# One batch row's decays through DRAM instead of TensorE, and a new written-out order, in a gated linear attention with a bilinear feed-forward layer

## The chip, the cores and the metric

The kernel runs on one core of a Trainium2 chip. TensorE (PE) multiplies matrices, VectorE (DVE), ScalarE (ACT) and GpSimd (POOL) work elementwise, SyncE (SP) issues transfers. The metric is the device time of one execution in microseconds (us).

## The reference, cut to what matters

Per batch row and head a 48 x 48 state is decayed, updated and read at each of 768 positions; the eight heads' outputs, side by side, go through a bilinear layer.

```python
# q, k, v, alpha: (4, 8, 768, 48); w_a, w_b: (384, 1536); w_out: (1536, 384)
for t in range(768):
    state = alpha[:, :, t, :, None] * state + k[:, :, t, :, None] * v[:, :, t, None, :]
    y[:, :, t] = (q[:, :, t, None, :] @ state)[..., 0, :]
x = y.transpose(0, 2, 1, 3).reshape(3072, 384)
out = ((x @ w_a) * (x @ w_b)) @ w_out
```

## The kernel before

**Chunks.** The work is cut into six chunks. Chunk `c` holds the 256 positions of third `c // 2` for two of the four batch rows, which are its rows `u` = 0 and 1. A partition holds two neighbouring positions (`r` = 0, 1), so a row is 128 partitions, and these are two halves `g` of 64 partitions. The recurrence is solved half by half: scores within a half, and a state carried from half to half.

**Attention, per row.** `la` is the logarithm of alpha and `l2` its sum over the two positions of a partition. A product with a triangular matrix gives running sums of `l2` in PSUM (`B` for chunk 0, which starts from `la` itself, `A2` elsewhere); ScalarE turns them into `beta` (their exponential) and `invb` (that of the negative sum) (`E`). VectorE multiplies q by `beta` and k by `invb` into `QKp` (`mq`, `mk`). `QKp` is transposed to `kqT`, by TensorE (`C`, evicted by `Ce`) in chunks 0 and 1 and by a transposing DMA (`T`) in the others. Scores are `D`, their masks `M`, or `Mc` and `Mm` in two steps, what a half adds to the state `K`, the state's update `k` (lines L758 to L762), the outputs from the state `SA` and `SB`, those from the scores `Y`, and `X` evicts the result as `xT`.

**The decay.** The update `k` of half `g` multiplies the state by the exponential of that half's whole sum, a number for each head and each of 48 rows of the state, with the rows on partitions (tile `bl`, two buffers that chunks take in turn). There are two ways to get it. In chunks 0 and 1, `dk` (L687) lets TensorE sum `l2` (in chunk 0: `la`) over the partitions of each half, one 48 x 2 product per head and row, and `de` (L692) takes the exponential. In chunks 2 to 5 the last partition of each half of `beta` already holds the numbers, in a row: `dr` (L671) writes them to DRAM by two transfers and `dl` (L676) reads them back, four bytes at a time, with the rows of the state on partitions, by two more. All four are issued by SP.

**The bilinear layer, per chunk.** `a f w` and `b f w` (L851) are the products of `xT` with block `f` of 12 of `wa_t` and `wb_t`, for one row (`w` = 0, 1, 256 columns) or both (`*`, 512 columns), three matmuls each. ScalarE copies `a` out of PSUM (`as`, L857), VectorE multiplies it by `b` into `prod` (`pr`, L865). `o m half` (L873) are six matmuls each with `wo_t`, `ot` evicts, `st` stores; the last block of tokens is done in two column halves (`oc`, `otc`, `stc`, L884).

**The order.** Nothing is scheduled by the compiler. `PROGRAM` is a list of such steps, each with its chunk; each engine runs its own instructions in the order of the list, and waits by semaphores for its operands and for the buffers that it writes. A digit at the end of a step that fills PSUM is the first of the banks that it takes, out of eight; a final letter names the engine: V VectorE, S ScalarE, P GpSimd, Y SP. Where it stands on a load (`ld`, of q, k, v or alpha as `a`), it is the queue that issues the transfer. `W` and `Wo` load the weights on GpSimd's queue. `fill n i` is `n` matmuls of zeros that nobody reads, put in to keep TensorE at work, and `cz`, `cs`, `cu`, `ci`, `cm` prepare constants. The list weaves the attention of a chunk into the bilinear layer of the chunk before.

Of the kernel before, what the change touches and what calls it, by code (L numbers as in the profile page):

```python
# [17 lines left out]
0: ld a 0b Y; cm 0; cz 0 q P; cz 0 b P; c1; cs 0 m V; c1a; ld a 0a Y; ld k 0b Y; ld q 0b Y; cu; ld q 0a Y; fill 7 6; cu2 P; ld v 0 P; cus; ld a 1 P; ln 0b  # L18
0: B 0b 5; ln 0a; ci; ld q 1 P; B 0a 0; E 0b i; E 0b b; ld k 0a Y; cz 1 b P; ld k 1 P; dk 0 3; mk 0b V; mq 0b V; E 0a b; C 0 1 4; cm 1; ld v 1 P; E 0a i
0: mq 0a V; W b 0 256; fill 3 1; mk 0a V; Ce 0 1 S; C 0 0 0; v 0 V; de 0; D 0 1 6; Ce 0 0 V; K 0 0 5; k 0 0 V; W a 0 256; M 0 1; D 0 0 4; SB 0 0; ln 1; W a 256 768  # L20
0: cz 0 v V; W b 256 768; M 0 0; B 1a 2
1: ld a 0 P
0: cs 1 0 P
1: ld a 1 P
0: B 1b 6; E 1a i; E 1a b; mq 1a V; mk 1a V; W a 768 1536; dk 1 5; E 1b i; C 1 0 2; de 1; v 1 S; mk 1b V; SA 0; Y 0; Ce 1 0 V; W b 768 1536; D 1 0 3
1: ld k 0 P
0: E 1b b; K 1 0 5; cs 1 m V; mq 1b V; X 0 S
1: ld v 0 P
0: K 0 1 2; C 1 1 6; a 0 0 0; a 1 0 7; Mc 1 0; k 0 1 V; Ce 1 1 V; k 1 0 V; a 2 0 3; as 1 0
1: ld q 0 P  # L30
0: cs 0 0 P; b 1 0 1; D 1 1 6; as 0 0; SB 1 4; Mm 1 0 V; as 2 0; Mc 1 1; a 3 0 0; pr 1 0; a 4 0 2; c2 P; Wo 0 6; cz 1 q V; Wo 6 12; b 2 0 3; pr 2 0; Mm 1 1 V
0: as 3 0; b 0 0 6; b 4 0 1; b 5 0 7; pr 0 0; Y 1; SA 1; K 1 1 6
1: ln 0
0: as 4 0
1: l2 0 V; ld k 1 P
0: X 1 S; b 3 0 0; a 5 0 2
1: ln 1
0: a 5 1 4; a 4 1 5; pr 3 0; pr 4 0; as 5 0; a 3 1 0; b 5 1 3
1: l2 1 V
0: pr 5 0; as 4 1; b 4 1 2; as 5 1; a 1 1 5; b 1 1 1; pr 4 1  # L40
1: ld q 1 P
0: cz 1 v P
2: ld a * P
0: as 1 1; a 6 * 4; as 3 1; pr 1 1
1: ra 0
0: a 0 1 0; a 2 1 7; a 8 * 1; b 3 1 2; pr 5 1; k 1 1 V
1: H 1 V; H 0 S
0: as 6 *
1: L 1 V
0: b 2 1 3; a 11 * 5; pr 3 1  # L50
1: L 0 V
0: a 7 * 6
1: ld v 1 P
0: as 11 *; b 6 * 2; as 2 1; pr 6 *; b 11 * 7; a 10 * 4
1: ra 1
0: as 0 1; pr 2 1
1: v 0 V
0: pr 11 *; as 7 *
1: lv 0 k P; A2 0 2
2: ld k * P  # L60
0: b 0 1 0
1: A2 1 5
0: as 8 *; b 7 * 3
1: lv 0 q V
0: pr 0 1
2: ld q * P
1: E 1 i; E 0 b
0: pr 7 *
1: E 1 b; E 0 i; mq 0 V
0: b 10 * 6; b 9 * 1; a 9 * 7; as 9 *; as 10 *  # L70
1: mk 0 V
0: b 8 * 0
1: dk * 5
0: pr 8 *; pr 10 *; pr 9 *
1: C 0 1 3; C 0 0 4
0: o 3 0 0
1: Ce 0 1 S; de *; Ce 0 0 V; K 0 0 7; D 0 0 4; k 0 0 V; K 0 1 3; D 0 1 1; Mc 0 0; lv 1 k P; SB 0 6; M 0 1
0: o 3 1 -
1: mk 1 V
0: o 0 0 5; ot 3 S  # L80
2: ln *
1: lv 1 q V
2: ld v * P
3: ld a * P
0: o 0 1 -
1: mq 1 V
0: o 2 0 4
1: Mm 0 0 V; k 0 1 V; C 1 0 2
0: o 1 0 0
1: Ce 1 0 V; v 1 V  # L90
2: l2 * V
0: ot 0 S; o 1 1 -
2: ra 0
1: SA 0
0: ot 1 S
2: H * S
1: D 1 0 1; K 1 0 3
2: lv 0 k P
1: M 1 0; Y 0
0: o 2 1 -  # L100
1: X 0 S; C 1 1 5
0: ot 2 S
1: a 5 0 6
2: L * V
1: Ce 1 1 V
2: lv 1 k P
1: a 3 0 1; k 1 0 V; as 3 0; a 1 0 0; as 5 0; b 1 0 7; b 3 0 2; as 1 0
2: A2 1 1
1: pr 3 0
2: ra 1  # L110
3: ld k * P
1: pr 1 0; SB 1 5
2: E 1 i
1: D 1 1 3; K 1 1 2; M 1 1
2: lv 1 q P; lv 0 q P; E 1 b
1: a 11 0 0
2: A2 0 7
1: as 11 0; b 11 0 1
2: E 0 i
1: b 5 0 0; pr 11 0  # L120
2: E 0 b
1: a 4 0 4; pr 5 0; a 0 0 3
2: dr
1: a 6 0 1; k 1 1 V; as 4 0; as 0 0; a 2 0 0; b 4 0 7
2: mk 1 V
1: as 6 0; b 6 0 3; pr 6 0; a 7 0 1; b 0 0 2; pr 4 0; b 7 0 4; pr 0 0; a 9 0 3; as 9 0
2: mq 1 V
1: as 2 0; SA 1; Y 1; as 7 0
2: T 1
1: b 9 0 2; X 1 S; pr 7 0; a 8 0 3; pr 9 0; b 2 0 0; as 8 0  # L130
2: v 1 S
1: b 8 0 1; pr 2 0; a 10 0 4; b 10 0 2
3: lv 0 k P
1: a 0 1 0
2: mq 0 V
1: as 10 0; a 9 1 5; as 0 1; pr 10 0; a 5 1 6
4: ld a * P
1: b 5 1 7
3: ln *
1: b 0 1 3; pr 8 0; a 2 1 0  # L140
2: dl
3: lv 1 k P
1: as 5 1; pr 0 1; a 1 1 2; b 1 1 4; as 1 1; pr 5 1; as 9 1; b 9 1 3; pr 1 1; as 2 1; a 8 1 6
2: mk 0 V
1: a 4 1 7; b 2 1 1
2: v 0 S
1: as 4 1; pr 9 1; a 11 1 2; b 11 1 0; b 4 1 5; pr 2 1; b 8 1 3; pr 4 1; as 8 1; pr 8 1
3: l2 * V
1: a 3 1 4
2: T 0  # L150
1: as 11 1; a 7 1 1; b 3 1 6
0: st 3 Y
1: o 2 0 5; a 10 1 7; as 7 1
3: ld q * Y
1: pr 11 1; as 3 1
0: st 1 Y
1: as 10 1; pr 3 1
2: D 1 0 3; K * 0 1; Mc 1 0; D 1 1 6; k * 0 V
1: a 6 1 0; b 7 1 2
3: ra 1  # L160
2: Mc 1 1
1: pr 7 1
5: ld a * Y
1: b 10 1 3; o 2 1 -; as 6 1
3: ra 0
0: st 0 Y
1: b 6 1 4; ot 2 S; pr 10 1
2: Mm 1 0 V; D 0 0 2; K * 1 1
3: H * V
1: pr 6 1; o 3 0 0  # L170
2: Mc 0 0; k * 1 V; Mm 1 1 V; SB 0 4; SB 1 6
3: L * V
2: D 0 1 2
3: lv 1 q P
1: o 0 0 1
2: Mc 0 1
1: o 3 1 -
2: Mm 0 0 V
4: ln *
3: A2 1 3  # L180
2: Mm 0 1 V; SA 1
3: ld v * P
4: ld v * P
2: Y 1; Y 0; X 1 V; SA 0
3: A2 0 2
2: X 0 S
3: E 0 b
1: o 0 1 -
3: lv 0 q V; E 1 b; E 0 i; mk 0 V
1: ot 3 S  # L190
3: E 1 i
2: b 5 * 6; b 3 * 4; a 4 * 5; a 5 * 7
1: ot 0 S
3: mq 1 V
2: a 3 * 2; a 2 * 1
3: dr
2: a 1 * 3; as 5 *; b 0 * 7; as 3 *; b 1 * 0; as 1 *
3: v 1 V
2: pr 5 *; pr 3 *; as 2 *
1: st 0 Y; st 3 Y  # L200
4: ld q * P
3: dl
2: b 2 * 3
3: mq 0 V
2: a 6 * 1
3: T 0
0: st 2 Y
2: as 6 *; pr 1 *
4: l2 * V; H * V; ra 1
2: as 4 *; b 4 * 2; a 11 * 0; b 6 * 6; a 0 * 4; b 8 * 1  # L210
1: o 1 0 5
4: L * V
2: pr 2 *; pr 6 *
3: v 0 V
2: as 0 *; a 8 * 3; pr 4 *; as 11 *; pr 0 *
3: mk 1 V
2: b 11 * 2; a 7 * 6; as 8 *; pr 11 *
1: o 1 1 -
2: pr 8 *
3: T 1  # L220
1: st 2 Y
3: K * 0 2
1: ot 1 S
3: k * 0 V
4: ld k * Y
1: st 1 Y
3: K * 1 0; D 0 0 3
2: as 7 *
3: Mc 0 0
2: b 9 * 1  # L230
3: k * 1 V
2: a 9 * 7
5: ld k * Y
2: b 10 * 5; as 9 *; a 10 * 6; b 7 * 3; pr 9 *; as 10 *; o 0 0 0; pr 7 *; pr 10 *
3: D 1 1 6; D 1 0 1
4: lv 1 k P
3: M 1 1
2: o 0 1 -
3: Mc 1 0
5: ld q * P  # L240
3: Mm 1 0 V; SB 0 3
2: ot 0 S
3: SB 1 1; D 0 1 5
4: lv 1 q V; A2 0 0
2: o 2 0 7
3: Mc 0 1
4: ra 0; lv 0 k V
5: ln *
4: E 0 b
3: Mm 0 1 V  # L250
2: o 3 0 6
3: Mm 0 0 V
5: lv 1 k P
4: lv 0 q P
5: ld v * P
3: Y 1; SA 0; Y 0; SA 1
2: o 3 1 -
3: X 0 S; X 1 V
2: o 2 1 -
4: mq 0 V; A2 1 2  # L260
2: ot 2 S
3: a 2 * 5
5: l2 * V
3: b 4 * 3
4: E 1 b; E 0 i; E 1 i
3: b 3 * 4; a 4 * 7; b 2 * 2
4: v 1 S
3: as 2 *
4: dr
5: H * S  # L270
2: ot 3 S
5: ra 0
2: st 0 Y
4: mk 0 V
3: as 4 *
4: mk 1 V
2: st 2 Y
3: a 8 * 1
4: T 0
3: a 1 * 0; a 0 * 6; b 8 * 7; as 8 *; b 5 * 5; pr 2 *; pr 4 *  # L280
4: v 0 V; dl
5: lv 0 q V
3: pr 8 *
4: mq 1 V
5: lv 0 k V
3: as 0 *
5: ra 1
3: a 3 * 1; a 5 * 3; b 0 * 7; a 9 * 6; as 5 *; pr 5 *; a 7 * 3; a 11 * 5; pr 0 *; as 9 *; as 3 *; as 1 *
4: T 1
3: b 9 * 6; b 1 * 1  # L290
5: lv 1 q V
3: pr 9 *; a 6 * 2; pr 3 *; as 11 *; pr 1 *; as 6 *
4: K * 0 0; D 0 0 4
5: L * V
3: as 7 *; b 11 * 6; b 6 * 7; pr 11 *; a 10 * 1; pr 6 *
4: Mc 0 0
2: o 1 0 5
3: as 10 *
4: k * 0 V; D 1 0 3; D 1 1 6; D 0 1 1
5: v 1 S  # L300
4: Mc 1 0; M 1 1
5: A2 0 0
2: o 1 1 -
4: SB 0 6; Mc 0 1; Mm 0 0 V; SB 1 3
2: ot 1 V
5: A2 1 2
3: b 7 * 1
5: E 1 i; E 1 b; E 0 b
3: b 10 * 5
4: Mm 0 1 V; Mm 1 0 V  # L310
3: pr 7 *; o 1 0 2
5: mk 1 V
3: pr 10 *; o 2 0 1
5: mq 1 V
4: Y 1; SA 0
5: dr
2: st 3 Y
5: T 1
4: Y 0; SA 1; X 1 S
5: E 0 i  # L320
3: o 1 1 -; o 2 1 -
4: X 0 V
5: mk 0 V; mq 0 V
3: ot 1 S
4: a 6 * 0; a 7 * 5; as 6 *
5: T 0
4: b 6 * 3; as 7 *; a 1 * 6
5: dl
4: pr 6 *; a 0 * 5; b 7 * 7; pr 7 *
3: ot 2 V; st 1 Y  # L330
4: as 0 *; as 1 *; a 5 * 3; b 1 * 4; b 0 * 2
2: st 1 Y
3: st 2 Y
4: pr 1 *; as 5 *; pr 0 *
5: v 0 V
4: a 3 * 0; a 4 * 7; as 3 *
5: D 0 0 5
4: as 4 *
5: K * 0 4; M 0 0; D 1 1 2; D 1 0 0; Mc 1 1
3: o 3 0 7  # L340
5: k * 0 V; Mc 1 0
3: o 3 1 -
5: SB 1 5
3: ot 3 S
5: SB 0 3; D 0 1 0
4: b 10 * 2
3: o 0 0 7
5: M 0 1; Mm 1 0 V; Mm 1 1 V
4: b 3 * 1; b 4 * 0
3: o 0 1 -  # L350
4: pr 4 *; b 5 * 0
3: ot 0 S
5: SA 1
4: pr 5 *
5: Y 1; Y 0
4: pr 3 *
5: X 1 V; SA 0
4: a 2 * 7; a 10 * 6
5: X 0 S
4: as 10 *; as 2 *; a 8 * 5  # L360
5: a 4 * 3
4: b 2 * 0
3: st 0 Y
5: a 2 * 4
4: pr 2 *; as 8 *; a 9 * 7
5: b 2 * 1; a 11 * 0
4: pr 10 *; b 8 * 5
5: as 2 *; as 4 *; a 1 * 4
4: b 9 * 2; pr 8 *
5: pr 2 *; b 5 * 3; b 1 * 6  # L370
4: as 9 *
5: b 4 * 1; a 8 * 5
4: a 11 * 7
5: pr 4 *
4: pr 9 *
5: b 11 * 1; as 11 *; as 1 *; a 5 * 4; a 0 * 2; pr 11 *; pr 1 *; as 0 *; as 5 *; b 0 * 0; b 7 * 6
4: o 0 0 1; as 11 *
# [31 lines left out]
def kernel(  # L409
# [14 lines left out]
    C = 128  # L424
# [599 lines left out]
```

## Time and profile before

| | |
|---|---|
| median of 3 runs | 196.53 us (195.69 to 196.65) |
| the profiled execution | 196.2 us, of which the profile's span is 194.4 us |
| PE busy | 189.4 us (97%), 2582 matmul records |
| DVE, ACT, POOL busy | 133.2, 106.4, 50.6 us |
| mean granted TensorE clock | 0.999 |
| moved by DMA | 29.40 MB in 57034 packets |

Times in the views count from the span's start. Matmul records are pipelined: one lasts longer than the distance to the next, so stretches of the chain of waits, which follow each other without overlap, are what costs are taken from. A group of the profile carries a line of the kernel and the tiles written and read. A matmul of 32-bit operands leaves two records in `dk` (two passes), so 16 of its matmuls are 32 records.

### The profile page before, as it was taken

To read this page: it belongs to the slowest core of one execution; us is meant where nothing else is said; L and a number is where in the kernel's file an instruction comes from. 1 tells how busy PE (TensorE), PEld (TensorE's weight loads), DVE (VectorE), ACT (ScalarE), POOL (GpSimd) and SP (SyncE) were. 2 spreads that over 40 slices of the span, in tenths; PEclk is the share of its full clock that TensorE was granted. 3 is DMA by queue.
4 is the path that set the end of the run, shared out by engine and by line. 5 is a ranking of instruction groups with operands and counts; after the bars stand their busy time and mean duration, and the time that the engine had idled before them with its cause. 6 is when DMAs were issued, how large, how long until landed. Compare 5 with 4: busy or idle time off the path is not lost.

```text
span 194.4 us, 5977 instructions
## 1 busy us (share of the span) xinstructions
PE 189.4 (97%) x2582; PEld 119.6 (62%) x2582; DVE 133.2 (69%) x221; ACT 106.4 (55%) x197; POOL 50.6 (26%) x69
## 2 busy tenths in 40 slices
PE   7999999999999999999999999999999999999993
PEld 3988875566888876644557544557455644445562
DVE  2498777988998879579786777996585525543311
ACT  4458784655859777645547684863462253431311
POOL 8999749160727004400004500000000000000000
PEclk9999999999999999999999999999999999999999
DMA  5999999999976999998699599007850100000342
GB/s 145 270 210 220 244 240 229 261 254 263 246 199 113 189 200 303 141 281 165 113 291 231 82 205 146 1 3 72 177 138 0 44 3 0 0 0 0 129 146 95
DMA packets 57034, 29.40 MB, mean 151 GB/s; under 512 B 47560, under 2 KB 54600, under 8 KB 57008
## 3 DMA queue, kind: packets, MB, share of 16 engines
q0 software_dynamic: 19056, 15.73, 44.0%
q1 hardware_dynamic: 37808, 13.19, 32.3%
q8 instruction: 20, 0.33, 0.7%
q10 hardware_dynamic: 144, 0.10, 0.2%
q14 instruction: 6, 0.05, 0.1%
HBM read 25.98 MB, written 4.74 MB: 158 GB/s over the span
## 4 chain that ended last, share of the span: by engine, by line
PE 96%; DVE 1%; issue 1%; ACT 0%; DVEq 0%
PE psum L851 48%; PE psum L873 24%; PE psum L797 7%; PE psum L773 3%; PE psum L744 2%; PE psum L628 2%; PE psum L707 2%; PE psum L571 2%; PE psum L588 2%; PE psum L589 2%; PE psum L687 1%; PE psum L884 1%; DVE kqT L715 0%; DVE m L786 0%; DVE prod L865 0%
## 5 line engine op out<-in xcount | busy, mean ns | idle before, releaser
L851 PE MATMUL psum<-xT,wb_t 128*128 128x512 bf16 (+1 forms) x270 | 56.0, 337 | 0.0
L851 PE MATMUL psum<-xT,wa_t 128*128 128x512 bf16 (+1 forms) x270 | 55.5, 337 | 0.0
L873 PE MATMUL psum<-wo_t,prod 128*128 128x384 bf16 x276 | 49.5, 326 | 0.0
L851 PEld LDWEIGHTS <-wa_t 128*128 128x128 bf16 x270 | 25.9, 98 | 19.6 <-issue 0.2
L851 PEld LDWEIGHTS <-wb_t 128*128 128x128 bf16 x270 | 25.7, 98 | 19.9 <-issue 0.6
L873 PEld LDWEIGHTS <-prod 128*128 128x128 bf16 x276 | 26.0, 98 | 18.2 <-issue 0.5
L888 ACT ACTIVATE ot<-psum 128x384 f32<-128x384 f32 (+1 forms) x20 | 9.5, 480 | 20.4 <-PE psum L873 16.1
L642 POOL TENSOR_TENSOR k_t<-k_t,a_t 128x384 f32<-128x384 f32 x8 | 8.5, 1069 | 38.7 <-DMA k_t<-in_k_dram 36.0
L782 ACT ACTIVATE m<-psum 128x1024 bf16<-128x1024 f32 x15 | 15.1, 1022 | 4.3 <-PE psum L773 4.3
L778 DVE TENSOR_TENSOR m<-psum,mask 128x1024 bf16<-128x1024 f32 x9 | 11.0, 1217 | 3.4 <-PE psum L773 3.3
L832 ACT ACTIVATE xT<-psum 128x768 bf16<-128x768 f32 x8 | 6.5, 810 | 9.6 <-PE psum L797 9.5
L554 ACT ACTIVATE la<-a_t 128x1536 f32<-128x1536 f32 (+2 forms) x9 | 9.5, 1054 | 3.5 <-DMA a_t<-in_alpha_dram 3.4
L786 DVE TENSOR_TENSOR m<-m,mask 128x1024 bf16<-128x1024 bf16 x15 | 11.2, 765 | 0.1
L666 DVE TENSOR_TENSOR QKp<-k_t,invb 128x768 bf16<-128x768 f32 x10 | 9.4, 951 | 2.3 <-issue 1.5
L797 PE MATMUL psum<-m,vx 64*64 64x128 bf16 x576 | 10.3, 217 | 0.2 <-DVE m L786 0.2
L773 PE MATMUL psum<-kqT 64*64 64x128 bf16 x384 | 10.0, 219 | 0.3 <-DVE Sm L758 0.2
L666 DVE TENSOR_TENSOR QKp<-q_t,beta 128x768 bf16<-128x768 f32 x10 | 9.7, 972 | 0.2
L797 PEld LDWEIGHTS <-vx 64*64 64x64 bf16 x576 | 9.0, 107 | 1.0 <-issue 0.8
L547 POOL DMA_DIRECT2D v_t<-in_v_dram x8 | 8.4, 1053 | 0.1
L773 PEld LDWEIGHTS <-kqT 64*64 64x64 bf16 x384 | 6.9, 106 | 2.4 <-issue 2.0
L797 PE MATMUL psum<-kqT,Sm 64*64 64x128 bf16 x144 | 7.9, 220 | 0.0
L642 POOL TENSOR_TENSOR q_t<-q_t,ra 128x384 f32<-128x384 f32 x4 | 4.1, 1024 | 14.1 <-DMA q_t<-in_q_dram 12.8
(262 smaller groups left out, 286.2 us busy)
## 6 DMA issues: line engine op xcount, KB each, us to landing
out_dram<-ot SPq DMA_DIRECT2D x23, 192.0 KB, 2.9
a_t<-in_alpha_dram POOLq DMA_DIRECT2D x3, 768.0 KB, 13.9
q_t<-in_q_dram POOLq DMA_DIRECT2D x3, 768.0 KB, 9.2
k_t<-in_k_dram POOLq DMA_DIRECT2D x2, 768.0 KB, 12.1
v_t<-in_v_dram POOLq DMA_DIRECT2D x4, 384.0 KB, 7.1
k_t<-in_k_dram SPq DMA_DIRECT2D x2, 768.0 KB, 6.6
a_t<-in_alpha_dram POOLq DMA_DIRECT2D x3, 384.0 KB, 8.9
q_t<-in_q_dram POOLq DMA_DIRECT2D x3, 384.0 KB, 13.5
```

The lines of the kernel that those rows point to most:

```text
L547: eng.dma_start(out=t[:, us, hs].rearrange("p b h r d -> p (b h) (r d)"), in_=src[ch.b0 + us.start:ch.b0 + us.stop, hs, ch.s * 2 * C:(ch.s ...
L554: nc.scalar.activation(out=ch.la[:, us, hs].rearrange("p b h r d -> p (b h r d)"), in_=ch.a[:, us, hs].rearrange("p b h r d -> p (b h r d) ...
L642: eng.tensor_mul(x, x, by)
L666: eng.tensor_mul(QKp[ch.c % 2][:, u, j, :, hs, :D], src[:, u, hs].rearrange("p h r d -> p r h d"), f)
L773: nc.tensor.matmul(s2[g * HC:(g + 1) * HC, r, p, rk, :], lhsT=ch.kqT[u][rs, 1, rk, 2 * h + p, g * HC:(g + 1) * HC], rhs=queriesT(ch, u, 2 ...
L778: nc.vector.tensor_mul(m.rearrange("p r a k s -> p (r a) (k s)"), ch.s2[u, h].rearrange("p r a k s -> p (r a) (k s)"), maskn(4))
L782: nc.scalar.activation(out=m.rearrange("p r a k s -> p (r a) (k s)"), in_=ch.s2[u, h].rearrange("p r a k s -> p (r a) (k s)"), func=AF.Copy)
L786: eng.tensor_mul(x, x, maskn(4))
L797: nc.tensor.matmul(y[c * DP:(c + 1) * DP, g, j // 2 * C:(j // 2 + 1) * C], lhsT=lhsT, rhs=rhs, start=(g, c) not in begun, stop=False, skip ...
L851: nc.tensor.matmul(p, lhsT=(wa_t, wb_t)[w][:, kk, f * 128:(f + 1) * 128], rhs=ch.xT[:, kk, us, :], start=(kk == 0), stop=(kk == KT - 1))
L873: nc.tensor.matmul(op, lhsT=ch.prod[:, f, at:at + C], rhs=wo_t[:, f, :], start=(f == 0), stop=(f == NFF - 1))
L888: nc.scalar.activation(out=o_, in_=i_, func=AF.Copy)
```

## The change

The decays of chunk 1 are split by row. Row 0 keeps the way through TensorE (`dk 0`, `de 0`, 8 matmuls, 16 records, where `dk *` had 16 matmuls, 32 records). Row 1 gets its decays by `dr 1` and `dl 1`: two transfers of one row of 384 numbers out of `beta`, and two of 48 x 8 numbers back. So that a row's decays lie together, the DRAM tile `row` and `bl` are laid out with the row first and the half second, and `dr`, `dl`, `de` and the update `k` address them so; chunks 2 to 5 still take both rows at once.

`PROGRAM` as a whole is another order of the steps. Apart from `dk`, `de`, `dr` and `dl` it holds the same attention and bilinear steps, some of them on another engine or queue or with the mask in the other form, and `fill 7`, `fill 3` have become `fill 5`, `fill 3`. Other functions that are added or changed (`rest`, `top`, `cum_quads`, `const_utb`) are called by no step of the list, and chunk 0 takes the same path through `expo` and `mul` as before.

```diff
 (the first steps, up to the first products of the bilinear layer)
-0: ld a 0b Y; cm 0; cz 0 q P; cz 0 b P; c1; cs 0 m V; c1a; ld a 0a Y; ld k 0b Y; ld q 0b Y; cu; ld q 0a Y; fill 7 6; cu2 P; ld v 0 P; cus; ld a 1 P; ln 0b
-0: B 0b 5; ln 0a; ci; ld q 1 P; B 0a 0; E 0b i; E 0b b; ld k 0a Y; cz 1 b P; ld k 1 P; dk 0 3; mk 0b V; mq 0b V; E 0a b; C 0 1 4; cm 1; ld v 1 P; E 0a i
-0: mq 0a V; W b 0 256; fill 3 1; mk 0a V; Ce 0 1 S; C 0 0 0; v 0 V; de 0; D 0 1 6; Ce 0 0 V; K 0 0 5; k 0 0 V; W a 0 256; M 0 1; D 0 0 4; SB 0 0; ln 1; W a 256 768
-0: cz 0 v V; W b 256 768; M 0 0; B 1a 2
...
-0: B 1b 6; E 1a i; E 1a b; mq 1a V; mk 1a V; W a 768 1536; dk 1 5; E 1b i; C 1 0 2; de 1; v 1 S; mk 1b V; SA 0; Y 0; Ce 1 0 V; W b 768 1536; D 1 0 3
...
-0: E 1b b; K 1 0 5; cs 1 m V; mq 1b V; X 0 S
...
-0: K 0 1 2; C 1 1 6; a 0 0 0; a 1 0 7; Mc 1 0; k 0 1 V; Ce 1 1 V; k 1 0 V; a 2 0 3; as 1 0
+0: cm 0; ld a 0b Y; ci; cz 1 b P; c1a; c1; cz 0 b V; cz 0 v V; cu; cu2 P; ld a 0a Y; fill 5 3; ld v 0 P; ld q 0b Y; ld k 0b Y; ln 0b; cus; ln 0a; B 0b 6
+0: cz 1 v V; cz 0 q V; cz 1 q V; E 0b b; E 0b i; B 0a 4; dk 0 6; ld a 1 P; ld q 1 P; ld k 1 P; ld k 0a Y; mk 0b V; E 0a b; mq 0b V; E 0a i; ld q 0a Y; mk 0a V
+0: C 0 1 7; cm 1; cs 0 m P; mq 0a V; fill 3 0; C 0 0 1; de 0; Ce 0 1 S; v 0 V; D 0 1 6; Ce 0 0 V; ld v 1 P; cs 0 0 P; ln 1; W a 0 256; K 0 0 3; k 0 0 V; W b 0 256
+0: D 0 0 2; SB 0 0; M 0 1; W a 256 768; cs 1 m P; W b 256 768; Mc 0 0; B 1a 4
...
+0: E 1a b; B 1b 2; dk 1 7; mq 1a V; mk 1a V; Mm 0 0 V; C 1 0 6; E 1b b; W a 768 1536; W b 768 1536; K 0 1 5; mq 1b V; E 1b i; Y 0; v 1 V; SA 0; mk 1b V; Ce 1 0 S
+0: de 1; C 1 1 4; D 1 0 6; k 0 1 V; Ce 1 1 V; X 0 S; Mc 1 0; K 1 0 5; a 1 0 0; k 1 0 V; as 1 0; a 0 0 4; D 1 1 2; SB 1 6; b 1 0 1; b 0 0 5; M 1 1; as 0 0
+0: pr 0 0; Mm 1 0 V; c2 P; a 5 0 0; a 2 0 4
...
+0: pr 1 0; b 5 0 2; a 3 0 5; as 5 0; a 4 0 3; as 2 0; pr 5 0; SA 1; b 2 0 1; Y 1; as 4 0; K 1 1 4; b 4 0 0; b 3 0 3
 (chunk 1's decays)
-1: dk * 5
...
-1: Ce 0 1 S; de *; Ce 0 0 V; K 0 0 7; D 0 0 4; k 0 0 V; K 0 1 3; D 0 1 1; Mc 0 0; lv 1 k P; SB 0 6; M 0 1
+1: dr 1; C 0 0 0; C 0 1 6
...
+1: dl 1
...
+1: lv 1 k P; Ce 0 1 S; dk 0 2; K 0 0 3; de 0
...
 (the functions)
-    bls = [cst.tile([C, B, P2], F32, name=f"bl{i}") for i in range(2)]
+    bls = [cst.tile([C, 2, 2, P2], F32, name=f"bl{i}") for i in range(2)]
...
-    def decay_rows(ch):
-        ch.row = row = dram.tile([2, 2 * P2, 2, D], F32, name="row")
+    def decay_rows(ch, us):
+        if not hasattr(ch, "row"):
+            ch.row = dram.tile([2, 2, P2, 2, D], F32, name="row")
         for g in range(2):
-            nc.sync.dma_start(out=row[g:g + 1].rearrange("g (b a) r d -> g b (a r d)", b=2),
-                              in_=ch.beta[(g + 1) * HC - 1:(g + 1) * HC].rearrange("g b h d -> g b (h d)"))
-
-    def decay_load(ch):
+            nc.sync.dma_start(out=ch.row[us, g:g + 1].rearrange("b g a r d -> g b (a r d)"),
+                              in_=ch.beta[(g + 1) * HC - 1:(g + 1) * HC, us].rearrange("g b h d -> g b (h d)"))
+
+    def decay_load(ch, us):
         for r in range(2):
-            nc.sync.dma_start(out=bls[ch.c % 2][r * DP:r * DP + D].rearrange("d b a -> d (b a)"),
-                              in_=ch.row[:, :, r, :].rearrange("g a d -> d (g a)"), allow_slow_non_contiguous=True)
+            nc.sync.dma_start(out=bls[ch.c % 2][r * DP:r * DP + D, us].rearrange("d b g a -> d (b g a)"),
+                              in_=ch.row[us, :, :, r, :].rearrange("b g a d -> d (b g a)"), allow_slow_non_contiguous=True)
...
-        bl = bls[i][:, 2 * g + us.start:2 * g + us.stop].rearrange("p b (a o) -> p b a o", o=1).broadcast_to([C, n, P2, D])
+        bl = bls[i][:, us, g].rearrange("p b (a o) -> p b a o", o=1).broadcast_to([C, n, P2, D])
```

SP's queue before issued nothing between the first six loads and chunk 2's `dr`. In the new order it issues, after the first six loads: chunk 1's `dr 1` and `dl 1`, the loads of q for chunk 2 and alpha for chunk 3, a store, chunk 2's `dr`, the load of alpha for chunk 4, chunk 2's transposes around its `dl`, and so on; of these loads GpSimd's queue issued those three before.

## The prediction

> **What bounds the kernel now.** I read the busy times first, then PE's waits, then the chain of waits in order of time, then the stretches, and last the DMA views that the new decays go through. Part 1 of the page, PE's waits (us in total, times, longest), and busy time by stretch (length, then PE, PEld, DVE, ACT, POOL):
>
> ```profile
> PE 189.4 (97%) x2582; PEld 119.6 (62%) x2582; DVE 133.2 (69%) x221; ACT 106.4 (55%) x197; POOL 50.6 (26%) x69
> ```
> ```profile
> PE psum L571 <- DVE og L475: 1.2, 1, 1.2
> PE psum L773 <- DVE Sm L758: 0.2, 1, 0.2
> PE psum L797 <- DVE m L786: 0.2, 1, 0.2
> ```
> ```profile
> 0.00:24.30 24.30, 22.64 (x417) 18.03 (x418) 15.44 (x34) 14.37 (x28) 21.42 (x42) 1.00 1.12 218
> 24.30:100.00 75.70, 75.70 (x1073) 51.12 (x1072) 63.26 (x109) 49.13 (x97) 23.89 (x23) 1.00 1.11 216
> 100.00:154.00 54.00, 53.92 (x891) 30.66 (x890) 40.85 (x59) 29.92 (x49) 5.25 (x5) 1.00 0.63 111
> ```
>
> From 24.3 us on TensorE never stops, and after its last matmul 3.2 us of eviction and store remain. So the end moves by what PE's list gains or loses after 24.3, and by how much of that list the first 24 us get done. The chain (start, length, what) prices both:
>
> ```profile
> 1.19 3.17 PE psum L571 x7
> 4.36 0.75 PE psum L588 x2
> 5.10 0.64 PE psum L589 x2
> 5.74 0.64 PE psum L588 x2
> 6.38 0.41 PE psum L589 x2
> 6.79 0.33 PE psum L588 x2
> ...
> 37.56 0.82 PE psum L687 x32
> ...
> 99.43 0.97 PE psum L873 x6
> 100.41 0.57 PE psum L773 x32
> 100.98 1.08 PE psum L873 x6
> 102.06 0.46 PE psum L797 x24
> 102.52 0.22 PE psum L773 x16
> ```
>
> Three things to see. The same matmuls of `B` take 0.32 us each before about 6.4 us and 0.16 after: the array starts at half speed. The decay products (L687) stand on the chain. And a visit to the small attention products costs something beside its work: six `o` matmuls (L873) take 0.97 us after their like but 1.08 after scores, and 16 scores 0.57 - 0.22 = 0.35 when they open a visit but 0.22 inside one. So a visit costs 0.13 + 0.11 = 0.24 us.
>
> **The change, part by part**, against the profiled execution (196.2 us: span 194.4 and 1.8 around it; the median of the runs lies 0.33 above it).
>
> *The matmuls removed.* Half of 32 records, 0.82 / 2 = 0.41 us, on PE where nothing waits: -0.41. `de` has half the columns, on ACT with its 55%: nothing.
>
> *The transfers added.* The update that needs them (`k 1 0`) is fixed by PE's list. From `A2 1`, whose sums make this row's `beta`, to `K 1 0` the new list has eight halves of `o` (7.8 us), five products of 512 columns (0.65 each: 3.2), seven of 256 (0.33: 2.3), four `C` (1.8), and about 4 of small work and visits: 19 us. ACT has up to 4 us queued ahead of that `beta`, so 15 are left. The same transfers for later chunks:
>
> ```profile
> L676 SPq DMA_DIRECT2D bl<-row x8: 337/543/1385, 61.1 to 140.6; - x8
> DMA to landing us min/median/max: 2.6/3.0/4.4
> ```
> ```profile
> SPq L676 <- DMA row<-beta: 2.7, 1, 2.7
> kqT<-QKp SPq DMA_TRANSPOSE x8, 6.1
> ```
>
> Two issues of `row` (0.6), a wait of 2.7, two issues of `bl` (at most 2.8) and a landing of at most 4.4 make 10.5 us, beside a DMA as full at 61 us as it will be at 40. Hidden: 0. Without that cover VectorE would stand at `k 1 0`, with `pr 5`, `pr 11` and chunk 2's `mk 1` behind it, and PE at `SB 1`. On SP, behind `dr 1` (waits for `beta`) and `dl 1` (waits for `dr 1`), stand the loads of q for chunk 2 and alpha for chunk 3, which GpSimd's queue issued at 33.8 and 42.4; issued near 43 and landing in some 6 us they are still 8 us ahead of their first readers. 0. The layouts move only addresses. 0.
>
> *The fills.* Seven end at 1.19 + 7 x 0.42 = 4.15 us, just when the first logarithm (ACT, 3.46 to 3.98) lets `B 0b` start. Five end at 3.30; `B 0b` starts no earlier. As work: 0. But PE then pauses 0.85 us while it is still slow, and full speed came 5.2 us after the first matmul (1.19 to 6.4). No row has a pause at half speed. If it does not count, nothing is lost. If the 5.2 us begin again at 4.15, full speed comes at 9.35 and all of `B 0a` runs slow: 8 x 0.16 = 1.3 us, straight into the chain `B`, exponentials, products, `C`. I take 0.6, a little under the middle, since the pause is a sixth of the 5.2 us.
>
> [...]
>
> *The first 24 us.* Up to `SB 0` the new order waits at the same places (the copy of `kqT`, the state update before `D 0 0`), and GpSimd's and SP's moved loads are bound by a DMA that is 9 tenths busy either way. The difference comes at row 1. Both orders have `B 1b` and `dk 1` done by 15.98 and `beta` of the first half by 14.75. VectorE then has, in the new order, `mq`, `mk`, a masking (0.68), `mq`, the cast of v (0.68, on ACT before), `mk`: 4 x 0.48 + 2 x 0.6 = 3.1, so `C 1 1` starts near 18.0, as before (18.07). But before, `D 1 0` and `K 1 0` were done by then; now they stand behind it: 0.22 + 0.24 + a visit's return 0.11, so the first bilinear product comes 0.55 later than 18.65. At 22.7 the old order waited 0.3 us for a mask; the new one waits a like time for a bank (`b 2` after `pr 1`, with a 1.2 us mask and two steps ahead on VectorE). It gains 0.15 by `SA 1` and `D 1 1` having fewer products ahead. +0.4, between 0 and 0.9.
>
> *Visits after that.* Counted in the lists, after the last attention step of chunk 0: 19 before, 20 now. +0.24.
>
> *Transposes.* Chunk 3's `T 1` now follows `mq 1` behind `pr 4`. From `b 4`'s end the list gives PE 7.0 us (one `a`/`b` of 0.65 for each of five, two halves of `o`, `K` twice, a score, `A2`, a visit) until `D 1 0`; VectorE needs 0.73 + 0.95 of them. That leaves 5.3 us for a landing whose median is 6.1, where the old order gave 7.0 (issue 93.3, use 100.3). Chunk 2's `T 1` has about 6.1. Ends: 0, if the landings are the shorter ones, and 1.8 if the landing takes 7.1, as the first did (59.05 to 66.2). I take 0.3, near the low end, since DMA is emptier after 80 us.
>
> Sum: -0.41 + 0.6 + 0.4 + 0.24 + 0.3 = +1.13: 197.3 for a profiled execution, 197.7 for the median.
>
> **The rivals.**
> *The pause costs nothing and transposes land in time.* Then -0.41 + 0.4 + 0.24 = +0.23, 196.8. For it: no gap inside the list ever slowed the clock again. Against it: those gaps were at full speed.
> *Faster: the first stage closes its holes.* By the prices of full speed PE has 1.7 us of empty time, visits aside, between 6.4 and 24.3 us. If the new order halves it, -0.85 - 0.17 = -1.0, 195.5. It decides if `C 1 1` starts before 17.6 and `b 2` meets a free bank: VectorE's casts and masks would have to be shorter than the 0.68 I gave them (some casts take 0.35). For it: the old order's waits at 11.3 and 22.7. Against it: VectorE has more to do there than before.
> *Much slower: SP's queue.* The decays or the transposes land as late as the rows allow, behind the loads that were moved onto SP: +1.8 in place of 0.3, 199.2. For it: in the old order, too, an update followed the landing of `bl` at once (70.1, 70.27). Against it: before, SP issued nothing between 3.9 and 55.2 us.
>
> **How the numbers follow.** The forecast (pause costs part or all of a window, rest as summed) has 0.45; cost-free pause 0.27; closed holes 0.14; SP's queue 0.14. A measurement of this kernel tells about 0.5% (1 us). Of the forecast's 0.45, whose own range is 197.1 to 198.4, 0.12 lies within 1 us; so slower is 0.33 + 0.14 + 0.01 = 0.48, within 0.5% is 0.12 + 0.25 + 0.01 = 0.38, faster is 0.13 + 0.01 = 0.14. The range runs from the closed holes (195.6) to the forecast with a full slow window and a late transpose (199.0), and leaves out the ends of two rivals.
>
> **What would show it.** L687 with 80 records, PE idle from 3.3 to 4.1, the `B` records going from 0.32 to 0.16 us later than 6.4, the first `xT` product near 19.2, no VectorE wait on DMA at chunk 1's second `L754`, a PE gap before chunk 3's scores near 101. Wrong I would be if `B` speeds up at 6.4 all the same, if the bilinear layer starts before 18.6, or if PE stands at the decays.

## The result, and the profile after

The changed kernel is slower: 198.72 us median of 4 runs (197.49 to 200.13) beside 196.11 us of the kernel before (4 runs, 195.69 to 196.65), a ratio of 1.0147, 95% interval 1.0109 to 1.0185. Its profiled execution is the shortest of the four: 197.49 us, 195.6 of them the span. In a second set of ten runs (`x_same` below) it was 1.0109 (1.0076 to 1.0143). Ratios leave disturbed runs out, medians do not, so the two can differ (most in `b_q`).

Busy time by engine (share, instructions), then PE's waits (us in total, times, longest), both of the changed kernel:

```profile
PE 189.6 (97%) x2564; PEld 119.9 (61%) x2564; DVE 136.0 (69%) x226; ACT 107.7 (55%) x194; POOL 43.9 (22%) x62
```
```profile
PE psum L558 <- DVE og L457: 1.2, 1, 1.2
PE psum L575 <- ACT la L540: 0.7, 1, 0.7
PE psum L793 <- issue: 0.5, 1, 0.5
```

The second line is the pause behind the five fills: `B` (L575) waits 0.7 us for the first logarithm. The third is new too, a stop of PE with no semaphore behind it. By stretch (length, then PE, PEld, DVE, ACT, POOL, clock, DMA share, GB/s):

```profile
0.00:25.16 25.16, 22.91 (x415) 18.34 (x416) 15.72 (x35) 14.62 (x28) 20.85 (x41) 1.00 1.13 218
25.16:100.00 74.84, 74.38 (x1044) 49.97 (x1045) 61.92 (x110) 50.50 (x96) 17.15 (x16) 1.00 1.08 199
```

The clock column rests on a record that begins only with full clock, so it does not show the slow start. The bilinear layer is dense from 25.16, where before it was from 24.31; and 0.46 us are now empty between 25 and 100, where before there was nothing. The chain (start, length, what) shows both places, and the shorter decay products:

```profile
4.25 0.98 PE psum L575 x2
...
7.14 0.64 PE psum L575 x2
7.78 0.42 PE psum L576 x2
8.20 0.33 PE psum L575 x2
...
39.32 0.46 PE psum L683 x16
...
79.36 0.51 PE psum L793 x26
79.87 0.47 issue
80.34 0.86 PE psum L793 x46
```

`B` takes 0.64 us for two records until 7.8 and 0.33 from 8.2 on: full speed comes 1.4 us later than before. Chunk 0's `dk` then starts at 8.85 instead of 8.09, 0.76 us late. At chunk 1, 16 decay records take 0.46 us where 32 took 0.82.

To place the difference, compare the two at the start of the dense part (24.31 and 25.16) and at the end of PE's last matmul (191.1 and 192.3). Up to the dense part the new order is 0.85 us late: the 0.76 of the clock and 0.09 of order. From there on the old order took 166.8 us and the new one 167.2, with 0.4 us of products fewer, so 0.8 us more went into visits and waits. Of these, 0.68 is the stop at 79.87, counted from the start of one product to the start of the next; the chain's 0.47 counts from the product's modelled end. 0.85 + 0.4 is about the 1.2 by which the spans differ. So in this execution the start and the stop account for the loss.

### The profile page after: what moved, and what is told of

The parts are those of the page before. It is cut to its first block, busy times and chain, and to the rows that moved or that the text cites. A ratio compares the mean times of both kernels' runs of the same rounds, so it can differ in the third digit from the quotient of the medians.

```text
span 195.6 us, 5961 instructions
## 1 busy us (share of the span) xinstructions
PE 189.6 (97%) x2564; PEld 119.9 (61%) x2564; DVE 136.0 (69%) x226; ACT 107.7 (55%) x194; POOL 43.9 (22%) x62
## 4 chain that ended last, share of the span: by engine, by line
PE 95%; DMA 1%; DVE 1%; ACT 0%; issue 0%
PE psum L847 49%; PE psum L869 24%; PE psum L793 7%; PE psum L769 3%; PE psum L740 2%; PE psum L575 2%; PE psum L703 2%; PE psum L621 2%; PE psum L576 2%; DMA a_t<-in_alpha_dram 1%; PE psum L683 1%; PE psum L880 1%; DVE kqT L711 0%; PE psum L558 0%; ACT la L540 0%
## 5 line engine op out<-in xcount | busy, mean ns | idle before, releaser
L635 POOL TENSOR_TENSOR k_t<-k_t,a_t 128x384 f32<-128x384 f32 x8 | 9.4, 1185 | 46.1 <-issue 25.2
L886 DVE COPY ot<-psum 128x384 f32<-128x384 f32 (+1 forms) x12 | 6.4, 537 | 12.0 <-PE psum L869 11.0
L884 ACT ACTIVATE ot<-psum 128x384 f32<-128x384 f32 (+1 forms) x13 | 6.2, 477 | 14.4 <-PE psum L869 12.9
L828 ACT ACTIVATE xT<-psum 128x768 bf16<-128x768 f32 x10 | 8.0, 810 | 7.5 <-PE psum L793 7.4
L661 DVE TENSOR_TENSOR QKp<-k_t,invb 128x768 bf16<-128x768 f32 x10 | 11.5, 1153 | 0.0
L661 DVE TENSOR_TENSOR QKp<-q_t,beta 128x768 bf16<-128x768 f32 x10 | 10.3, 1032 | 0.5 <-ACT beta L650 0.3
L782 DVE TENSOR_TENSOR m<-m,mask 128x1024 bf16<-128x1024 bf16 x15 | 9.9, 684 | 0.0
L769 PE MATMUL psum<-kqT 64*64 64x128 bf16 x384 | 9.5, 219 | 0.3 <-DVE Sm L754 0.2
L635 POOL TENSOR_TENSOR q_t<-q_t,ra 128x384 f32<-128x384 f32 x3 | 3.0, 997 | 27.2 <-DMA q_t<-in_q_dram 14.3
```

The lines of the kernel that those rows point to most:

```text
L635: eng.tensor_mul(x, x, by)
L661: eng.tensor_mul(QKp[ch.c % 2][:, u, j, :, hs, :D], src[:, u, hs].rearrange("p h r d -> p r h d"), f)
L769: nc.tensor.matmul(s2[g * HC:(g + 1) * HC, r, p, rk, :], lhsT=ch.kqT[u][rs, 1, rk, 2 * h + p, g * HC:(g + 1) * HC], rhs=queriesT(ch, u, 2 ...
L782: eng.tensor_mul(x, x, maskn(4))
L828: nc.scalar.activation(out=o_, in_=i_, func=AF.Copy)
```

## The experiments

Theory A: the loss is the pause between the fills and `B`, through the moment at which the array comes to full speed. Rival B: the pause is harmless and the loss lies behind it, in the order or in the transfers. `x...` kernels are edits of the changed kernel, `b...` of the kernel before.

### The changed kernel again, and with seven fills

`x_same`, no edit:

> The changed kernel again, unaltered, beside the same runs of the kernel before as the others. It says how far its time moves by itself: its four runs so far lie 2.6 us apart (197.49 to 200.13), those of the kernel before only 1 us. Theory A (the pause between the fills and the first B products makes the moment of full speed late, and by how much changes from run to run): median near 198.7, spread above 1.5 us, and in this profile B reaches 0.16 us a product at another time than 8.0 us. Theory B (the pause costs nothing, the loss lies in what follows): the change from slow to fast B products comes at 8.0 again, and the time that differs is found after 25 us.

`x_fill7`:

```diff
-... cu2 P; ld a 0a Y; fill 5 3; ...
+... cu2 P; ld a 0a Y; fill 7 3; ...
```

> Seven fills at the start in place of five, nothing else. Theory A: the two fills cover 3.3 to 4.15 us, full speed comes near 6.4 us as in the kernel before, C of the first half moves 0.76 us earlier, and the time falls by at least 0.8 us, to 197.9 or below, with a spread of 1 us. Theory B: the same time as the changed kernel within 0.3 us, since B's start is set by the first logarithm either way.

On one chip, beside the same runs of the kernel before: `x_same` 198.61 us (196.46 to 199.96), 1.0109; `x_fill7` 195.84 us (195.09 to 197.38), 0.9999 (0.9973 to 1.0025). Two matmuls of zeros, 0.85 us long, are worth 2.8 us by the medians and 2.2 by the ratios. Theory A, that the pause costs the time, holds, and its size was more than I had expected. With the fills in, the new order with its transfers is as fast as the kernel before, no faster. In the profile of `x_same` full speed came at 8.1 again, and the stop at 79.87 was not there: its span is 195.0. That sign of the profile is the one named for theory B; the median and the spread are those of theory A.

### The pause alone, in the old order

`b_fill5` has `fill 5 6` for `fill 7 6`.

> The kernel before with five fills at the start in place of seven, nothing else: the pause alone. Theory A: slower by 0.8 us or more (196.9 to 198.5), with a wider spread than the kernel before. Theory B: the same within 0.3 us (196.1).

197.05 us, 1.0069 (1.0042 to 1.0097). Full speed came at 8.6 in its profile, `dk 0` 1.03 us late. The edit costs about 1 us in the old order, more in the new one.

### Do fills ahead of a pause count at all?

`x_fill0` takes `fill 5 3` out. `x_late5` starts the five later, so that no pause is left:

```diff
-... ci; cz 1 b P; c1a; c1; cz 0 b V; cz 0 v V; cu; ...
+... ci; cz 1 b P; c1a; cz 0 b V; cz 0 v V; c1; cu; ...
```

> The changed kernel without any fills at the start. Theory A (activity ahead of a pause counts for nothing): the same time as with five fills, 198.6 within 0.5 us, and B reaches full speed at 8.0 us or later in the profile. Rival (activity adds up over a pause): full speed comes later by the 2.1 us that the five fills lasted, and the time rises by 1 us or more, to 199.6 or above.

> The changed kernel with its five fills started 0.77 us later (two zeroings of VectorE are put ahead of the zeros that the fills read), so that they end near 4.1 us and the pause is gone; the number of fills is unchanged. Theory A: the loss is gone, 195.8 to 196.6, with a spread of 1 to 1.5 us. Rival (the earlier start or the number of fills is what counts): 198.6 as before.

`x_fill0` took 198.91 us, 1.0112 (1.0073 to 1.0152): the same as with five fills ahead of a pause. By the time they had counted for nothing. One sign of theory A missed: in its profile (a run of 197.93) full speed came at 7.1, not at 8.0 or later. `x_late5` took 196.77 us, 1.0028 (1.0004 to 1.0052), a little above what was expected: with the same five fills and no pause, most of the loss is gone. That activity begins 0.8 us later than with seven may be what leaves a rest; no run separates this. So it is the pause more than the number. But the profile of `x_late5`, of a run of 196.87, has full speed at 8.0, as the changed kernel's has: what is shown is that the pause costs time, not that the moment of full speed sets the time of each execution.

A further execution of the changed kernel, `x_again`, shows the delay at its longest:

> The changed kernel unaltered, one more look. In its ten timed runs two lie near 196.6 and eight between 198.2 and 200.0; both profiles so far are of the shorter kind, with full speed at 8.0 us. [...] Rival: B is as in the shorter kind, and the 2 us are lost in holes of PE after 25 us.

197.56 us. The chain of `x_again`, and then that of the second execution with seven fills (`x_fill7_2`, below):

```profile
9.01 0.64 PE psum L576 x2
9.65 0.84 PE psum L683 x32
```
```profile
4.36 0.67 PE psum L575 x2
5.03 0.33 PE psum L576 x2
```

In the first, `B` runs slow to its last record at 9.6; in the second it is at full speed almost from its start. This is the same code in the same place. Full speed in all profiles, as the start of the first `B` record at the short distance:

| start | full speed at, us |
|---|---|
| seven fills' work from 1.2, a pause of at most 0.3 (eight profiles) | 4.6, 4.7, 4.9, 5.2, 5.8, 5.9, 6.1, 6.6 |
| five from 2.0, no pause | 8.0 |
| five from 1.2, pause 3.3 to 4.2 (four profiles, one of them in the old order) | 8.0, 8.1, 8.6, later than 9.1 |
| none, `B` from 4.2 | 7.1 |

The traces also hold a record of the granted clock. Its stretch at full clock begins where `B` changes its pace (at 6.42 us in the kernel before, 7.84 in the changed one).

The mean with seven fills is 5.5; with the pause it is past 8.4. The 3 us between them are more than three times the 0.85 us of the two fills, and no run shows what sets them. What the runs show is that with seven fills the moments are spread over 2 us (4.6 to 6.6), that five fills ahead of a pause bring no earlier moment than none (8.0 and later beside 7.1), and that in `x_fill0` full speed came 2.9 us after the first product (4.15 to 7.05), where in the kernel before it took 5.2 from the first matmul.

What is not settled: the three profiled executions of the changed kernel lie between 196.8 and 197.6 us, eleven of the twelve others between 198.1 and 200.1. No profile shows one of those. `x_again` was meant to be of the longer kind and took 197.56; in it even the latest moment of full speed costs only 0.7 us of span against `x_same`, so that moment alone, up to 9.6, doesn't explain 199.

### The transfers alone, in the old order

`b_dr1` has the new layout and functions with the old list, and

```diff
-1: E 1 b; E 0 i; mq 0 V
+1: E 1 b; E 0 i; dr 1; dl 1; mq 0 V
-1: dk * 5
+1: dk 0 5
-1: Ce 0 1 S; de *; Ce 0 0 V; ...
+1: Ce 0 1 S; de 0; Ce 0 0 V; ...
```

> The old order with the decays of chunk 1's row 1 by the two transfers in place of half of its 32 products, and the decay tile laid out by row; order, fills and queues as before otherwise. Theory 1 (transfers hidden behind 15 us of other work): -0.41 us from 16 fewer products, 195.7, and no engine waits for the transfers. Rival: the update of VectorE that reads them waits, since the old order reaches it earlier: 0 or slower, 196.1 to 197.5.

197.27 us, 1.0062 (1.0040 to 1.0083): the rival. From `b_dr1`, VectorE's wait (us in total, times, longest) and the answer for the tile `bl` between 30 and 60 us:

```profile
DVE Sm L773 <- DMA bl<-row: 1.2, 1, 1.2
```
```profile
DMA to landing us min/median/max: 9.9/9.9/9.9
```

The 1.5 KB of each transfer took 9.9 us here, where in the kernel before twice as much, for both rows of a later chunk, lands in 2.6 to 4.4. The last was issued at 42.3, behind loads of v, k and q that GpSimd's queue had issued from 30.6 to 33.6 and that landed from 45.2 to 51.6. In the changed kernel the two were issued at 43.0 and 43.3, landed by 49.1, and were read at 55.63. The same edit is late in one order and 6.5 us early in the other.

The profile of `b_dr1` also shows PE's stop without a semaphore, longer than in the changed kernel:

```profile
77.26 1.13 PE psum L812 x72
78.39 0.95 issue
79.34 0.86 PE psum L812 x48
```

By count of matmul records this is after number 1246 of the program. The changed kernel's stop comes after number 1246 as well, in another order; so are a short one in `x_fill7` and one of 1.3 us in `x7_dl`. A second place, number 1630, which is 3 x 128 matmuls (768 instructions with their weight loads) further, shows 0.55 us in `b_dr1` and 0.7 in `b_q`. These lengths count from start to start. `b_pad` moves what stands there and leaves the order:

```diff
-... ld q 0a Y; fill 7 6; ...
+... ld q 0a Y; fill 23 6; ...     (156 columns each, not 512)
```

> The old order with the two transfers (16 products fewer), and its seven fills of 512 columns cut into 23 of 156 columns: the same busy time at the start, but 16 products more ahead of everything else, so that every later product has the same place in PE's stream of instructions as in the kernel before. In the profile without them PE stood 1.16 us at its product 1246 and 0.55 us at product 1630, inside runs of small products and with no semaphore to wait for; the changed kernel stood 0.68 us at the same number 1246. Theory of the instruction stream (such a stop comes when a block of instructions arrives late; where it falls depends on what stands at that place of the stream): the two stops go or shrink to the 0.3 us of the kernel before, and the time falls by about 1 us from 197.27, to 195.9 to 196.5. Rival (the stops come from the load on the DMA that the transfers make): 197.2, with the same stops.

Both stops are gone from its profile (196.21 us for that execution, against 197.37), but the median stays at 197.25, 1.0045 (1.0017 to 1.0074), where 195.9 to 196.5 was expected. And the profile has another stop of the same kind, at an earlier place:

```profile
20.66 0.91 PE psum L867 x7
21.57 0.85 issue
22.42 0.41 PE psum L867 x2
```

By count, to within one, it lies seven times 128 matmuls ahead of number 1246, and among products of 256 columns; `x7_dl` has a shorter one there. So the reading that the stops belong to places of the stream is borne out. What they cost in the median of `b_dr1` is not shown, since `b_pad` has a stop as well.

`b_q` takes the load out of the decays' way:

```diff
-2: ld q * P
...
-1: E 1 b; E 0 i; dr 1; dl 1; mq 0 V
+1: E 1 b; E 0 i; dr 1; dl 1
+2: ld q * Y
+1: mq 0 V
```

> The old order with the two transfers, and the load of q for chunk 2 moved from GpSimd's queue (issued at 33.9) to SP's, behind the new load of decays. Theory (the decays landed 9.9 us after issue because three loads of 768 KB and 384 KB were ahead of them): they land by 49.5 instead of 52.4, VectorE's wait of 1.2 us at the second row's update goes, and the time falls from 197.27 to 195.6 to 196.2. Rival (what is lost in the old order is the stops in PE's stream at products 1246 and 1630): the wait goes and the time stays at 196.8 or above.

The decays landed at 48.9, 7.4 us after their issue and as expected, and the wait was gone; yet the ratio was 1.0105 (1.0067 to 1.0143), 197.8 us beside the 195.78 of the kernel before (the median of all its runs is 199.71, 196.71 to 202.11). The theory missed. The rival's number came true (the wait gone, the time above 196.8), but its profile, of a run of 196.94, has no stop at 1246 and only the 0.7 us at 1630, besides a wait of PE for a transposition (0.5). Why the old order with the transfers loses 0.5 to 1% stays open: without the wait for the decays the time did not fall, and each of the three profiles has a stop somewhere.

### The transfers and the decays of chunk 3, in the new order with seven fills

`x7_dkpe` gives row 1 back to TensorE; `x7_dl` moves a later load of decays ahead of a transposition on SP:

```diff
 (x7_dkpe, beside fill 7)
-1: dr 1; C 0 0 0; C 0 1 6
+1: C 0 0 0; C 0 1 6
-1: dl 1
-1: lv 1 k P; Ce 0 1 S; dk 0 2; K 0 0 3; de 0
+1: lv 1 k P; Ce 0 1 S; dk * 2; K 0 0 3; de *
 (x7_dl, beside fill 7)
-3: T 0
+3: dl; T 0
...
-3: dl
```

> The changed kernel with seven fills, and with chunk 1's row 1 decays by 16 products of TensorE again in place of the two transfers: the transfers alone, in the new order. Theory (hidden in the new order: they land at 49.3 us and are read at 55.6): 16 products more, +0.41 us over the 195.84 of the changed kernel with seven fills, so 196.1 to 196.4. Rival (the transfers cost as much as they save, by what they do to other transfers or to PE's stream of instructions): 195.5 to 195.9.

> The changed kernel with seven fills, and chunk 3's load of decays put ahead of its first transposition on SP. In the profile with seven fills the row was in DRAM at 86.8, but the load was issued at 91.7, behind the 4.2 us that the transposition takes on SP, and landed at 99.8: VectorE stood 1.7 us at the state update, and PE lost 0.7 us in the scores behind it. Theory: the load is issued near 87, lands by 94, that wait is gone, and the median falls by 0.3 to 0.7 us to 195.1 to 195.5. Rival (the transposition, 1.4 us later, becomes what PE waits for before chunk 3's first scores, or the loads of v and alpha on GpSimd's queue delay both): 195.8 to 196.8.

`x7_dkpe` took 198.16 us, 1.0119 (1.0085 to 1.0153), far more than 16 products. Its PE list is the same up to 37 us, but against `x_fill7_2` PE is 1.8 us late by 34 us, 0.8 of it from the start. PE's waits of `x7_dkpe`, then SP's queue (start, length, what) of `x7_dkpe` and of `x_fill7_2`:

```profile
PE psum L846 <- DMA wb_t<-in_moe_w_b_dram: 1.0, 1, 1.0
```
```profile
3.43 13.87 SPq L532 DMA_DIRECT2D q_t<-in_q_dram  x2
42.02 0.37 SPq L532 DMA_DIRECT2D a_t<-in_alpha_dram  x1
```
```profile
36.56 0.60 SPq L667 DMA_DIRECT2D row<-beta  x2
41.74 0.89 SPq L672 DMA_DIRECT2D bl<-row  x2
42.78 0.40 SPq L533 DMA_DIRECT2D q_t<-in_q_dram  x1
```

Without `dr 1` and `dl 1` nothing on SP waits for `beta`, so the second load of q in the first line, 768 KB for chunk 2, goes out near 17 us as soon as its buffer is free. It then shares the DMA with the weights: the last part of `wb_t` lands at 31.1 instead of 29.1, and PE waits for it. With the transfers, the same load is issued at 42.8. In the new order they are also the gate that holds SP's loads back. The price of the 16 products could therefore not be read from this pair.

`x7_dl` took 196.97 us, 1.0045 (1.0025 to 1.0065), no gain. What was to be removed is this wait of `x_fill7`:

```profile
DVE Sm L758 <- DMA bl<-row: 1.7, 1, 1.7
```

It is gone (the load was issued at 87.7 and landed at 91.2), but PE stood 1.3 us after product 1246 in the same profile. Neither expectation names that, and the median is above `x_fill7`'s, measured on another chip; so `x_fill7` was run again:

> The changed kernel with seven fills, once more and on whatever chip comes. Its first result (195.84 us, 0.9999 of the kernel before) was had beside five fills; the two kernels that build on it were had elsewhere, at 1.0045 (load of chunk 3's decays earlier) and 1.0119 (row 1's decays by TensorE). Theory (the start is what the changed kernel lost; what builds on it differs by its own edit): 0.998 to 1.003 again, so TensorE's 16 products cost far more than their 0.41 us in the new order. Rival (the new order's time depends on how fast the transfers of a run are, since it has little to spare at chunk 3's q, at the decays and at the weights; the differences between calls are mostly that): 1.003 to 1.008, with waits for transfers in the profile, and nothing can be said of the 16 products from kernels of different calls.

195.88 us, 0.9996 (0.9975 to 1.0017), on another chip. The first result stands, and with the fills the whole loss of the changed kernel is gone. No version beat the kernel before: the best, `x_fill7`, equals it.

## Why the prediction was right or wrong

The forecast of 197.7 us (195.6 to 199.0) held the median of 198.72, and the sign was right. The profiled execution was summed to 197.3 and took 197.49; that agreement is luck, since three terms of the sum were too dear and a stop of 0.68 that is not in it took their place. By its steps:

- **The fills**, +0.6: the step that failed, by size. The profile shows +0.76 at `dk 0`; with and without the two fills the medians differ by 2.8 us (2.2 by the ratios), 1 us in the old order. "I take 0.6, a little under the middle, since the pause is a sixth of the 5.2 us" supposed that the activity ahead of the pause counts for the rest. By the time it counts for nothing (`x_fill0`), and the moment of full speed moved by 1.4 us in this profile and 3 us in the mean. With all of `B 0a` slow, 1.3 in place of 0.6, the sum is 198.4, nearer to the median. But 1.3 us is the most that a slow `B 0a` explains by the prediction's own sum: the pause is shown to cost 2.2 to 2.8 us, and the path of what goes beyond the slow `B` stays open. The chances and the range speak of a window; no run shows one. The runs showed full speed 3.4 to 5.4 us after the first matmul with seven fills, 6.8 or more with five and the pause, and 2.9 us without any.
- **The matmuls removed**, -0.41: at their place 0.82 us became 0.46, -0.36.
- **The transfers added**, 0: they were hidden, with 6.5 us to spare. But the bound was wrong: SP waited 4.6 us for the row where I had 2.7, the load took 5.8 to 5.9 where I had "at most" 4.4, in all 11.5 us from first issue to last landing where 10.5 was to be the most. The durations came from 61 us on, and the step took the DMA to be as full there as at 40; the landings of 5.8 here and 9.9 in `b_dr1` do not fit that. The cover, 18 us from issue to use where I counted 15 behind the wait for `beta`, saved the step. That the loads behind them on SP cost nothing held, and in `x7_dkpe`, with the load of q out near 17 us, `wb_t` lands 2.0 us later and PE waits 1.0 for it.
- **The first 24 us**, +0.4: +0.09 in the profile. `D 1 0` and `K 1 0` do stand behind `C 1 1` (18.52 `C`, 19.14 `D`, 19.49 `K`, 19.73 the first bilinear product), but the bank of `b 2` was free.
- **Visits**, +0.24: `x_same`, without the stop, takes 166.5 us from its dense part (25.18) to its last matmul (191.7), 0.3 less than the old order with 0.4 of products fewer. At most 0.1 of the 0.24 shows.
- **Transposes**, +0.3: no gap near 101 us; chunk 3's landed at 101.9 and was read at 102.8.

So the fills were forecast too cheap, and the steps after them too dear by 0.8 together. Of the rivals, the costless pause is excluded. The first stage's holes did not close (order +0.09, though no wait for a bank). SP's queue is real but not where I put it: in profiles with an earlier start VectorE waits up to 1.7 us (`x_fill7`) and 2.2 us (`x_fill0`) for chunk 3's decays; in the changed kernel's own profile it does not.

## What to carry to other kernels

Here the matmuls of zeros at the start were worth their place only where they reached, with hardly a pause, to the first real product, and two of them were worth more (2.2 to 2.8 us) than the 16 products that the change saves (0.36). A small transfer took 9.9 us for 1.5 KB at 42 us behind loads of v, k and q (`b_dr1`), 7.4 with the load of q behind it (`b_q`), and 2.6 to 4.4 for 3 KB from 61 us on, so its bound has to come from rows at the same load. And its waiting place on a queue may be what holds large loads back from something more urgent: here q's 768 KB were issued at 42.8 instead of near 17 us, and the weights landed 2.0 us earlier. Where executions of one kernel differ by 2%, one profile, often the shortest, shows only part of the loss: repeat the kernel and take the edit out.

## What I had not expected of the hardware

PE stopped at the same places of its instruction stream in several kernels: after matmul 1246 in the changed one, `b_dr1`, `x_fill7` and `x7_dl`, after 1630 in `b_dr1` and `b_q`. These stops, and that of `b_pad`, have no semaphore behind them and end 1.3 to 1.5 us after the end of one packet of 16,384 bytes on the instruction queue: in the changed kernel the packet lasts from 77.7 to 78.9 and the stop ends at 80.34; in `b_dr1` 76.7 to 77.9 and 79.34; in `b_pad` 19.8 to 21.0 and 22.42. Those at 1246 and 1630 lie in runs of small products (15 to 20 ns apart), that of `b_pad` does not. The changed kernel has 20 such packets and 5128 matmuls and weight loads; if these are what the packets carry, 256 to a packet. Only one of its 20 packets has a stop of over 0.5 us in the 2.5 us behind it; the longer of the stops named above last 0.55 to 1.3 us. That a late packet is the cause was not shown: I infer it from the same numbers in different orders and from the packets, and no run took the DMA's load away.
